# Late rows of segments 62 and 63 projected in the opening, feed-forward products in steps 58 to 60, and the tail's transfers in another order

## The chip, the cores and the metric

The kernel runs on one core of one Trainium2 chip. The metric is the device time of one execution in microseconds (us), as the median of several runs. One further execution was taken with the hardware profiler; its instruction trace and a page made from it are what "the profile" means here. The engines are TensorE (PE for its matmuls, PEld for its weight loads), VectorE (DVE), ScalarE (ACT), GpSimd (POOL) and SyncE (SP). SP issues most transfers (DMAs) from one queue in program order; they are moved by 16 transfer engines.

## The reference

Part A is a transformer layer over 64 segments of 32 tokens with a recurrent memory of 8 rows; part B is a gated feed-forward layer over all 2,048 tokens. Numbers are bf16, the width D is 640, there are 32 heads of 128, and F is 1,728.

```python
mem = mem0                                    # [8, 640]
for s in range(64):
    h = concat([mem, LN(x)[32 * s:32 * s + 32]])           # 40 rows
    q, k, v = h @ Wq, h @ Wk, h @ Wv                       # 32 heads of 128
    p = softmax(where(mask, q @ k.T * 128 ** -0.5, -1e9))  # memory rows see all, the others causally
    o = (p @ v) @ Wo                                       # back to 640
    mem, out[32 * s:32 * s + 32] = o[:8], o[8:]            # the memory of the next segment
h = x + out
z = LN(h)
result = h + (relu(z @ W_gate) * (z @ W_up)) @ W_down
```

The loop over s is sequential: a segment's memory rows come out of the segment before it.

## The kernel before

**Scheduling.** The kernel writes its operations in one list (`add`, `dma`) with the tiles that each reads and writes as keys. `solve` works out the semaphore waits from the keys. Each engine runs its own operations in the order of the list, and SP issues its transfers in that order too: a transfer that must wait holds all transfers behind it.

**A step.** Segment s is one pass of the loop `for s in range(1, NSEG)`; the opening does segment 0. Of a segment's 40 rows, 32 (8 memory rows and the first 24 tokens, the "act_r" rows) are projected in the step itself, as the stationary operand of 128x32, while 512 columns of the weights stream past; four such matmuls go into the four 32-column groups of the array. The last 8 tokens of a segment don't depend on the memory. They are collected for four segments at a time (`act_e`, 32 rows), and their K, Q and V are projected ahead, in three of every four steps. `extra_units(s)` gives such a step its 40 additional matmuls, which `filler(0..2)` spreads over the places in the step where the recurrence would leave TensorE idle, and an `evac` that brings the result from the PSUM banks BQ (0 and 1) to `Ke`, `Qe` or `Ve`. `place(s)` says which of two buffers, and which slot of four, a segment has. Segments 0 and 1 have slots 2 and 3 of buffer 1, whose other two slots are empty in the opening; 62 and 63 have slots 0 and 1 and get their late rows' K, Q and V in steps 58, 59 and 60. Step 61 projects segment 63's remaining queries.

`merge_v` copies V (`Vp`, `Ve`) into VM by transfers, since rows change partitions; `pv_x(s - 1)` reads VM in the step after. `store_attn` writes the rows of attention to `attn_d`. `fill_of(s)` splits some of a step's matmuls in two halves of 256 columns, or shares fewer weight loads, so that each step has a chosen number of TensorE instructions.

**Feed-forward.** Tokens go in four blocks of 512. The first block's normalised rows are made during the steps and kept in `xn2_d`; step 62 loads them into `xn2T[0]`. `gate_up(b, j)` is one pair for 128 of the F columns: five matmuls of the gate and five of up (128x128 stationary, 512 tokens streaming), then `relu` on ScalarE and the product on VectorE into `hT[b % 2][:, j]`; j = 13 is a tail of 64 columns in `Wt`. `down_pair` multiplies `hT` by `Wd`; its first part of a block reads j = 0 to 11 and so the first four `Wd` loads at once. Block 0's pairs j = 0 to 3 stand in and behind the last step, where they fill waits of the recurrence; j = 4 to 13 follow in the loop of block 0.

**The tail's transfers.** The feed-forward weights lie where Wq, Wk and Wv were, so they can be loaded only after the last projection by each (`Wdone`). `load_piece` takes the next of a list of column groups of gate and up (`GROUPS`: 0 to 255, 256 to 511, 512 to 1,023, 1,024 to 1,535, 1,536 to 1,663), and `load_down` a third of the rows of `Wd` at a time. Each is tied to a key such as `("hT", 0, j)`, the product of pair j, which sets when SP may issue it. `ln2_load`, `ln2_front` and `ln2_back` load, normalise and turn the rows of the next block.

## Time and profile before

| | us |
|---|---|
| median of 3 runs | 1000.11 (1000.02 to 1000.35) |
| the profiled execution | 999.84 |
| its span, first to last instruction or transfer | 998.1 |
| TensorE busy with matmuls | 974.4 (98% of the span) |
| VectorE, ScalarE, GpSimd busy | 713.6, 524.3, 167.4 |

Busy time of TensorE is modelled from pipelined matmuls, so a busy TensorE isn't one at its peak; the chain of waits says better what sets the end. In the rows of groups, "xN" is the count, then come the busy time and the mean of one instruction in ns, then idle time before it. In the timeline and the chain, the first two columns are start and length in us. In the tables of stretches the last columns are the granted clock of TensorE, the mean busy share of the transfer engines, and GB/s.

### The profile page before, as it was taken

What the parts mean: (1) busy time and instruction counts of PE and PEld (TensorE: products, weight loads), DVE (VectorE), ACT (ScalarE), POOL (GpSimd) and SP (SyncE); (2) the same over time, 40 slices, a digit from 0 to 9 for tenths busy, and PEclk for the clock granted to TensorE, in tenths of its full rate; (3) what the DMA queues carried; (4) which work ended last, traced back from release to release, by engine and by line L of the source; (5) the groups of instructions that cost most, each with busy time, mean ns of one, the idle gap of its engine ahead of it and who ended that gap; (6) DMA issues with size and microseconds to landing.
All of it is one profiled execution on the core that took longest, in us unless ns stands there. A gap on an engine that the chain in (4) does not pass through costs nothing.

```text
span 998.1 us, 56128 instructions
## 1 busy us (share of the span) xinstructions
PE 974.4 (98%) x26025; PEld 533.0 (53%) x24736; DVE 713.6 (71%) x1861; ACT 524.3 (53%) x1330; POOL 167.4 (17%) x414
## 2 busy tenths in 40 slices
PE   3899999999999999999999999999999999999998
PEld 1145555655555555555556565655555554344443
DVE  2568787878888887888788878787878766345332
ACT  0456666656666666666666566665656643122120
POOL 7021202021302130222022212121110010000000
PEclk9999999999999999999999999999999999999999
DMA  9931212121222122121212131112111169513100
GB/s 373 416 109 28 54 28 54 30 60 51 54 42 54 49 54 46 48 55 48 49 46 61 45 60 42 41 41 39 41 36 39 35 181 249 101 20 93 27 14 26
DMA packets 73534, 73.32 MB, mean 73 GB/s; under 512 B 42480, under 2 KB 60112, under 8 KB 71376
## 3 DMA queue, kind: packets, MB, share of 16 engines
q1 hardware_dynamic: 71568, 68.83, 25.0%
q8 instruction: 199, 3.26, 1.4%
q10 hardware_dynamic: 1728, 0.91, 0.3%
q14 instruction: 39, 0.32, 0.1%
HBM read 37.04 MB, written 6.55 MB: 44 GB/s over the span
## 4 chain that ended last, share of the span: by engine, by line
PE 94%; DMA 3%; DVE 1%; SPq 1%; issue 0%; ACT 0%; DVEq 0%; ACTq 0%
PE ps L394 47%; PE ps L858 11%; PE ps L367 8%; PE ps L582 7%; PE ps L599 7%; PE ps L642 4%; PE ps L1114 3%; DMA W<-in_A_Wv_dram 3%; PE ps L483 2%; PE ps L671 2%; PE ps L536 2%; SPq L332 1%; PE ps L871 0%; PE ps L1127 0%; PE ps L894 0%
## 5 line engine op out<-in xcount | busy, mean ns | idle before, releaser
L394 PE MATMUL ps<-W,act_r 128*32 128x512 bf16 (+1 forms) x8327 | 453.7, 357 | 1.7 <-ACT tok L418 0.9
L394 PEld LDWEIGHTS ps<-W,act_r 128*32 128x32 bf16 x8327 | 213.9, 96 | 165.7 <-DVE act_r L623 32.1
L418 ACT ACTIVATE tok<-ps 128x512 bf16<-128x512 f32 x190 | 109.3, 594 | 57.3 <-PE ps L394 48.7
L394 PE MATMUL ps<-W,act_e 128*32 128x512 bf16 x1224 | 119.5, 383 | 5.9 <-DVE TBf L464 3.4
L413 DVE STREAM_TRANSPOSE Ko<-tox 128x512 bf16<-128x512 bf16 x128 | 89.5, 700 | 40.1 <-ACT tox L418 39.7
L491 POOL COPY Qo<-Qe 128x256 bf16<-128x256 bf16 x64 | 27.8, 434 | 528.6 <-DVE oT L556 488.9
L418 ACT ACTIVATE tox<-ps 128x512 bf16<-128x512 f32 x134 | 79.6, 598 | 63.2 <-PE ps L394 42.5
L562 DVE STREAM_TRANSPOSE oT<-tox 128x512 bf16<-128x512 bf16 x128 | 95.6, 747 | 0.0
L413 DVE STREAM_TRANSPOSE Qo<-tok 128x512 bf16<-128x512 bf16 x124 | 85.5, 690 | 0.9
L367 PE MATMUL ps<-W,act_e 128*32 128x512 bf16 x856 | 84.1, 384 | 0.0
L582 PE MATMUL ps<-Wo,oT 128*32 128x160 bf16 x4032 | 81.4, 233 | 0.0
L599 PE MATMUL ps<-Wo,oT 128*32 128x320 bf16 x2016 | 79.8, 299 | 0.6 <-DVE rm L546 0.6
L582 PEld LDWEIGHTS ps<-Wo,oT 128*32 128x32 bf16 x4032 | 70.3, 97 | 11.0 <-DVE oT L556 3.1
L418 ACT ACTIVATE Vp<-ps 128x512 bf16<-128x512 f32 x127 | 75.2, 592 | 0.5 <-PE ps L858 0.5
L886 ACT ACTIVATE g<-ps 128x512 bf16<-128x512 f32 x52 | 30.1, 593 | 79.3 <-PE ps L858 79.3
L612 ACT ACTIVATE SA<-TA 64x40 f32<-64x40 f32 x126 | 29.5, 234 | 75.3 <-DVE TA L610 74.5
L499 ACT ACTIVATE Pm<-ps 128x64 bf16<-128x64 f32 x126 | 28.1, 223 | 73.0 <-PE ps L483 72.9
L858 PE MATMUL ps<-xn2T,Wg 128*128 128x512 bf16 x260 | 64.7, 380 | 0.0
L858 PE MATMUL ps<-xn2T,Wu 128*128 128x512 bf16 x260 | 64.6, 379 | 0.0
L887 DVE TENSOR_TENSOR hT<-g,ps 128x512 bf16<-128x512 bf16 x52 | 35.7, 686 | 40.3 <-PE ps L858 38.4
L599 PEld LDWEIGHTS ps<-Wo,oT 128*32 128x32 bf16 x2016 | 52.7, 97 | 16.8 <-DVE rm L546 1.3
L556 DVE STREAM_TRANSPOSE oT<-om 128x128 bf16<-128x128 bf16 x126 | 39.0, 310 | 31.1 <-ACT om L548 31.1
(114 smaller groups left out, 1447.0 us busy)
## 6 DMA issues: line engine op xcount, KB each, us to landing
VM<-Vp SPq DMA_DIRECT2D x126, 65.0 KB
VM<-Vp SPq DMA_DIRECT2D x63, 130.0 KB
W<-in_A_Wk_dram SPq DMA_DIRECT2D x5, 1024.0 KB
W<-in_A_Wq_dram SPq DMA_DIRECT2D x5, 1024.0 KB
W<-in_A_Wv_dram SPq DMA_DIRECT2D x5, 1024.0 KB
Wo<-in_A_Wo_dram SPq DMA_DIRECT2D x8, 640.0 KB
attn_d<-wtok SPq DMA_DIRECT2D x248, 7.5 KB
xt<-in_A_x_dram SPq DMA_DIRECT2D x16, 160.0 KB
```

The source lines that it names most:

```text
L367: return pe.add_instruction(mybir.InstMatmult(name=nc.get_next_instruction_name(), engine=mybir.EngineType.PE, ins=[pe.lower_ap(rhs), pe.l ...
L394: ins = pe.matmul(*b, start=(c == ends[0]), stop=(c == ends[1]), skip_group_check=True)
L413: add("dve", lambda v: v.transpose(dst[:, 16 * i:16 * i + 16, 0:32], tok[t][:, :].rearrange("p (h f) -> p h f", f=32)), r=tok_keys(t), w=keys)
L418: add("act", lambda a: a.activation(dst, src, ACTF.Copy), r=r, w=w)
L556: add("dve", lambda v: v.transpose(ap(oT[par], 160 * hf, [[40, 4], [320, 4], [1, 8]]), ap(om, 128 * hf, [[1, 4], [4, 32]])), r=[("om", hf) ...
L562: add("dve", lambda v, kh=kh: v.transpose(ap(oT[p], 160 * kh + M, [[320, 4], [40, 4], [1, 32]]), ap(tox, 128 * kh, [[256, 4], [1, 4], [4, ...
L582: i = pe.matmul(bank(bk)[32 * gg:32 * gg + 32, 0:160], src[:, hb, 0:32], w[:, gg], start=(hb == CH[16 * halves[0]]), stop=(hb == CH[-1]), ...
L599: i = pe.matmul(bank(bk)[32 * q:32 * q + 32, 0:320], src[:, hb, 0:32], w, start=(n == 0), stop=(n == 7), skip_group_check=True)
L642: ins = pe.matmul(bank(bk)[32 * q:32 * q + 32, 0:320], src[:, hb, 0:32], w[:, 2 * (q % 2):2 * (q % 2) + 2], start=(i == 0), stop=(i == 15) ...
L858: ins = pe.matmul(bank(bk), w[:, c, lo:lo + 128], xn2T[par][:, c, :], start=(c == 0), stop=(c == DC - 1))
L886: add("act", lambda a: a.activation(g1[gi][:, :], bank(bg), ACTF.Relu), r=[B(bg)], w=[("g1", gi)])
L887: add("dve", lambda v: v.tensor_tensor(hT[par][:, j, :], g1[gi][:, :], bank(bu), ALU.mult), r=[B(bu), ("g1", gi)], w=[("hT", par, j)])
```

## The change

1. **Late rows.** `place` gives segments 0 and 1 slots 0 and 1 of buffer 1, and segments 62 and 63 slots 2 and 3. The opening loads the last 64 rows of x behind the first 64 in `xt`, normalises 128 rows, and puts the late rows of all four segments into `act_e[1]`. So the opening's projections give K, Q and V of the late rows of 62 and 63 too. Step 1 stores the buffer (`ends`, which now holds `Ke[1]`, `Qe[1]` and `Ve[1]` side by side) to `ends_d`; step 61 loads it back. One of the four loads of the memory moves from ACT's queue to SP's.
2. **Early products.** In steps 58 to 60 `extra_units` returns `early_product`: the gate and up products of block 0 for one j of 0, 1, 2 each. The normalised rows are loaded into `ends` in step 57, the weights into `xt` and `xl` (one j at a time), and the result goes to `hx_d`, which the tail loads into `hT`. These matmuls, and those of block 0's j = 3 to 6, go in four groups of 32 columns (`by_groups`). `fill_of` has new numbers for steps 58 to 60.
3. **Tail.** Block 0's pairs in and behind the last step are j = 3 to 6 in place of 0 to 3, and its loop has seven pairs (j = 7 to 13, counted as p = 4 to 10) in place of ten. The column groups are 384 to 639, 640 to 895, 896 to 1,407, 1,408 to 1,663, and last 0 to 383. `Wt`, `Wd`, the rows of h, the weights of columns 0 to 383 and the rows of block 1 are asked for at other pairs than before.

The core of the diff:

```diff
+    ends_d = nc.dram_tensor("ends_d", [128, 64 * H + 8 * VW], BF16)
+    NE = 3
+    hx_d = nc.dram_tensor("hx_d", [128, NE, TB], BF16)
...
-    Ke = [ar.alloc(f"Ke{i}", [128, H, 32], BF16) for i in range(2)]
+    ends = ar.alloc("ends", [128, 64 * H + 8 * VW], BF16)
+    Ke = [ar.alloc("Ke0", [128, H, 32], BF16), _Part(ends, 0, (H, 32))]
     Qo = ar.alloc("Qo", [128, H, M + SEG], BF16)
-    Qe = [ar.alloc(f"Qe{i}", [128, H, 32], BF16) for i in range(2)]
-    Ve = [ar.alloc(f"Ve{i}", [128, 8, VW], BF16) for i in range(2)]
+    Qe = [ar.alloc("Qe0", [128, H, 32], BF16), _Part(ends, 32 * H, (H, 32))]
+    Ve = [ar.alloc("Ve0", [128, 8, VW], BF16), _Part(ends, 64 * H, (8, VW))]
...
         if b < 0:
             for e in range(2):
-                copy(act_r[1][:, 2 + e, :, M:32], src[:, :, SEG * e:SEG * e + RID], [("act", 1, "x", 2 + e)])
-                copy(act_e[1][:, :, M * (2 + e):M * (3 + e)], src[:, :, SEG * e + RID:SEG * e + SEG], [("acte", 1)])
+                copy(act_r[1][:, e, :, M:32], src[:, :, SEG * e:SEG * e + RID], [("act", 1, "x", e)])
+            copy(act_e[1][:, :, :].rearrange("p c (e t) -> p c e t", t=M),
+                 src[:, :, :].rearrange("p c (e t) -> p c e t", t=SEG)[:, :, :, RID:SEG], [("acte", 1)])
...
     def place(s):
+        if s < 2 or s >= NSEG - 2:
+            return 1, s % 4
         return (s - 2) // 4 % 2, (s - 2) % 4
...
-    ln1_load(-1, xt, ("xt",), "act")
+    for n, t0 in enumerate((0, S - 64)):
+        dma(xt[64 * n:64 * n + 64, :], x_ap[t0:t0 + 64, :], w=[("xt", "late") if n else ("xt",)], eng="act")
     ln1_load(0, x0, ("oTe", 0), "act")
-    for g in range(4):
+
+    def mem_load(g, eng):
         dma(wtok[32 * g:32 * g + M, :, :],
-            mem0_ap.rearrange("t (c g j) -> g t c j", g=4, j=32)[g], r=[("wtok",)], w=[("wtok0", g)], eng="act")
+            mem0_ap.rearrange("t (c g j) -> g t c j", g=4, j=32)[g], r=[("wtok",)], w=[("wtok0", g)], eng=eng)
+
+    for g in range(3):
+        mem_load(g, "act")
     srcs = (A_Wq, A_Wk, A_Wv)
     for j in (1, 0, 2):
         for c in range(DC):
             dma(W[:, j, c, :], srcs[j][128 * c:128 * c + 128].rearrange("p h e -> p (h e)"), w=[("W", j, c)])
+            if j == 1 and c == 0:
+                mem_load(3, "sp")
...
+    EC = 128 * NE
+    GROUPS = ((EC, EC + 256), (EC + 256, EC + 512), (EC + 512, EC + 1024), (EC + 1024, FM), (0, EC))
     pieces = [(t, n, src, g, lo, hi) for g, (c0, c1) in enumerate(GROUPS)
               for n, (t, src) in enumerate(((Wg, B_W_gate), (Wu, B_W_up)))
-              for lo, hi in (((0, 3), (3, DC)) if c1 - c0 == 512 else ((0, DC),))]
+              for lo, hi in (((0, 3), (3, DC)) if g in (2, 4) else ((0, DC),))]
...
+    END_KEYS = [("Ke", 1, 0), ("Ke", 1, 1), ("Qe", 1, 0), ("Qe", 1, 1), ("Ve", 1, 0), ("Ve", 1, 1), ("Ve1", 1)]
+    XHOME = [(ends[:, 512 * c:512 * c + 512], END_KEYS[c]) for c in range(DC)]
+    HOME, HKEY = ends[:, 64 * H + 4 * VW + 8:64 * H + 4 * VW + 520], END_KEYS[DC]
+
+    def by_groups(pe, dst, w, x, c):
+        for g in range(4):
+            ins = pe.matmul(dst[32 * g:32 * g + 32, :], w[:, 32 * g:32 * g + 32], x, start=(c == 0), stop=(c == DC - 1),
+                            skip_group_check=True)
+        return ins
+
+    def early_rows(lo, hi):
+        dma(ends[:, 512 * lo:512 * hi].rearrange("p (c t) -> p c t", t=512), xn2_d[:, lo:hi, :],
+            r=[("xn2_d", u) for u in range(4)], w=END_KEYS[lo:hi] + ([("Ve1", 1)] if hi == DC else []))
+
+    def early_weights(j, q):
+        t, k, src = ((xt, ("xt",), B_W_gate), (xl, ("xl",), B_W_up))[q]
+        dma(chunks_of(t[:, :]), src[:, 128 * j:128 * j + 128].rearrange("(c p) f -> p c f", p=128), w=[k])
+
+    def early_product(s, n):
+
+        def mul(q, chunks):
+            t, k = ((xt, ("xt",)), (xl, ("xl",)))[q]
+
+            def f(pe):
+                for c in chunks:
+                    ins = by_groups(pe, bank(BQ[q]), chunks_of(t[:, :])[:, c, :], XHOME[c][0], c)
+                return ins
+            add("pe", f, r=[k] + [XHOME[c][1] for c in chunks], w=[B(BQ[q])])
+
+        def part(m):
+            mul(*((0, range(DC)), (1, range(1)), (1, range(1, DC)))[m])
+
+        def evac():
+            add("act", lambda a: a.activation(HOME, bank(BQ[0]), ACTF.Relu), r=[B(BQ[0])], w=[HKEY])
+            add("dve", lambda v: v.tensor_tensor(HOME, HOME, bank(BQ[1]), ALU.mult), r=[B(BQ[1]), HKEY], w=[HKEY])
+            dma(hx_d[:, n, :], HOME, r=[HKEY], w=[("hx", n)])
+        return part, evac
...
+        elif 2 <= s < NSEG - 3 and r < 3:
             j = (1, 0, 2)[r]
             a, ks = act_e[p], [("acte", p)]
-            if s < 0 or (s - 2) // 4 + 1 > (NSEG - 2) // 4:
-                return None, None
+            if (s - 2) // 4 + 1 == (NSEG - 2) // 4:
+                return early_product(s, r)
...
+                    if b == 0 and j < NE + 4:
+                        ins = by_groups(pe, bank(bk), w[:, c, lo:lo + 128], xn2T[par][:, c, :], c)
+                        continue
...
-        n = {1: 31, 2: 8, 57: 39, 61: 39, 62: 50, 63: 0}.get(s, FILL[s % 4])
+        n = {1: 31, 2: 8, 57: 39, 58: 0, 59: 27, 60: 40, 61: 39, 62: 50, 63: 0}.get(s, FILL[s % 4])
...
+            if NSEG - 6 < s < NSEG - 3:
+                early_weights(s - NSEG + 6, 1)
+            elif s == NSEG - 3:
+                for n in range(2):
+                    dma(ends[:, 1024 * n:1024 * n + 1024], ends_d[:, 1024 * n:1024 * n + 1024], r=[("ends",)],
+                        w=END_KEYS[2 * n:2 * n + 2])
+            elif s == 1:
+                dma(ends_d[:, :], ends[:, :], r=END_KEYS, w=[("ends",)])
...
+            if s == NSEG - 7:
+                early_weights(0, 0)
+                G.ops[-1].after = first_exp
+                early_rows(2, 4)
+            elif s == NSEG - 3:
+                dma(ends[:, 2048:], ends_d[:, 2048:], r=[("ends",)], w=END_KEYS[4:])
...
+        if s == NSEG - 7:
+            early_rows(0, 2)
+            early_rows(4, DC)
+            early_weights(0, 1)
+        elif NSEG - 6 <= s < NSEG - 4:
+            early_weights(s - NSEG + 7, 0)
...
     rows(P3, s % 2, s - 1)
-    gate_up(0, 1)
+    gate_up(0, NE + 1)
     load_piece(("VM", 0, 3))
-    load_piece(("hT", 0, 0))
+    load_piece(("hT", 0, NE))
     pv_x(s, P0)
     norm_x(P0)
     norm_x_late(P0)
     flip_ox(s)
     late_o(s)
-    load_piece(("hT", 0, 1))
-    gate_up(0, 2)
+    load_piece(("hT", 0, NE + 1))
+    gate_up(0, NE + 2)
     ln2_load(4)
-    load_piece(("hT", 0, 2))
-    load_piece(("hT", 0, 2))
-    gate_up(0, 3)
-    load_piece(("hT", 0, 3))
-    load_piece(("hT", 0, 3))
+    load_piece(("hT", 0, NE + 2))
+    load_piece(("hT", 0, NE + 2))
+    gate_up(0, NE + 3)
+    load_piece(("hT", 0, NE + 3))
+    dma(hT[0][:, 0:NE, :], hx_d[:, :, :], r=[("Wdone", 2), ("hT", 0, NE + 3)] + [("hx", n) for n in range(NE)],
+        w=[("hT", 0, n) for n in range(NE)])
     rows(P2, (s + 1) % 2, s)
     ln2_load(5)
     woe_pass(P3, range(16))
...
         if 0 < b < NBLK - 1:
             for u in range(4):
                 ln2_load(4 * (b + 1) + u)
-        at0 = 5 if b == 0 else 1
         for j in range(FC):
-            if b or j > 3:
+            p = j - NE if b == 0 else j
+            if b or p > 3:
                 gate_up(b, j)
-            if b == 0 and 4 <= j < 7:
-                load_piece(("hT", 0, j))
-            if b == 0 and j in (5, 7):
-                ln2_load(6 + (j - 5) // 2)
-            if b == 0 and 4 <= j < 9:
-                load_down(j - 4)
-            if b == 0 and j == 5:
+            if b == 0 and p == 4:
                 for q, src in enumerate((B_W_gate, B_W_up)):
                     for e in range(2):
                         r0 = FR * (q ^ e)
                         dma(Wt[:, e, :, r0:r0 + FR], src[:, FM:F].rearrange("(c p) f -> p c f", p=128),
-                            r=[("Wdone", 0), ("hT", 0, 5)], w=[("Wt", q, e)])
-            if b == 0 and j == 9:
+                            r=[("Wdone", 0), ("hT", 0, j)], w=[("Wt", q, e)])
+            if b == 0 and p in (5, 7):
+                ln2_load(6 + (p - 5) // 2)
+            if b == 0 and 4 <= p < 8:
+                for n in ((0,), (1, 2), (3,), (4,))[p - 4]:
+                    load_down(n, p)
+            if b == 0 and p == 6:
                 dma(h_rows[0][:, :, :], h_d[:, :].rearrange("(u p) d -> p u d", p=128), r=[("h_d", u) for u in range(4)] +
-                    [("Wdone", 1), ("hT", 0, 9)], w=[("h", 0, u) for u in range(4)])
+                    [("Wdone", 1), ("hT", 0, j)], w=[("h", 0, u) for u in range(4)])
+            if b == 0 and p in (8, 9):
+                load_piece(("hT", 0, j))
+                load_piece(("hT", 0, j))
             if b + 1 < NBLK:
-                if j - at0 in (0, 2, 4, 6):
-                    ln2_front(4 * (b + 1) + (j - at0) // 2)
-                if j - at0 - 2 in (0, 2, 4, 6):
-                    ln2_back(4 * (b + 1) + (j - at0 - 2) // 2, None)
+                fronts, backs = ((4, 6, 8, 10), (6, 8, 10, 10)) if b == 0 else ((1, 3, 5, 7), (3, 5, 7, 9))
+                if p in fronts:
+                    ln2_front(4 * (b + 1) + fronts.index(p))
+                for n in range(4):
+                    if p == backs[n]:
+                        ln2_back(4 * (b + 1) + n, None)
         assert not pieces
         for n in range(2):
             down_pair(b, n)
```

40 lines of the change are left out of this document (24 added, 16 removed).

## The prediction

> **What bounds the kernel now.** I read the page first, then the chain of waits of the whole run, then the timeline and tables of stretches of the three places that the change touches: the opening, steps 57 to 61, and the tail.
>
> ```profile
> span 998.1 us, 56128 instructions
> PE 974.4 (98%) x26025; PEld 533.0 (53%) x24736; DVE 713.6 (71%) x1861; ACT 524.3 (53%) x1330; POOL 167.4 (17%) x414
> PE 94%; DMA 3%; DVE 1%; SPq 1%; issue 0%; ACT 0%; DVEq 0%; ACTq 0%
> ```
>
> TensorE is 94% of the chain that ended last. So matmuls taken out of its stream come off the end, unless something is late at the place where they were. The chain's pieces (start, length, what) price them:
>
> ```profile
> 12.12 28.10 DMA W<-in_A_Wv_dram
> ...
> 809.89 2.27 PE ps L858 x10
> ...
> 814.68 2.26 PE ps L858 x10
> ...
> 826.18 19.53 PE ps L858 x90
> ...
> 845.71 1.09 PE ps L871 x10
> ```
>
> L858 is `gate_up`: ten matmuls of 512 columns make one pair. Nine pairs of block 0 in a row took 19.53 us, 2.17 us each. The single pairs in the last step took 2.26 and 2.27. The one DMA piece is the opening: the chain stands on a load of Wv until 40.22 us.
>
> **The pairs.** `GROUPS` and the loop over `p` leave block 0's gate and up products for j = 0 to 2 out of the tail; their results come back from `hx_d`. Off the chain: 3 x 2.17 = 6.51 us. In their place `early_product` puts 20 gate and 20 up matmuls of 32 columns into each of steps 58 to 60, where the late rows of segments 62 and 63 were projected:
>
> ```profile
> L394 PE MATMUL ps<-W,act_e 128*32 128x512 bf16 x72 | 7.0, 379 | 0.0
> ...
> L367 PE MATMUL ps<-W,act_e 128*32 128x512 bf16 x48 | 4.7, 379 | 0.0
> ...
> 746.73 0.35 PE ps L671 x32
> ...
> 758.77 0.35 PE ps L671 x32
> ...
> 770.81 0.35 PE ps L671 x32
> ...
> 808.81 1.08 PE ps L394 x20
> ```
>
> The first two rows, groups of 746.6 to 782.8 us, are the old work: 120 matmuls of 128x512 in 32 columns, 40 a step, as many as the new. A run of 20 such matmuls, each with its own weights, took 1.08 us in the chain (last row), so 40 take 2.16: one full pair. The new forty need 40 weight loads where the old shared 24; the split halves (`fill_of`: 7, 52, 56 become 0, 27, 40) shrink by 48, as much as the loads grow. The steps with 7 and 52 splits both last 12.04 us (the three L671 rows). I take 0 for both edits. ScalarE and VectorE get less: one activation and one product in place of two copies and up to two flips.
>
> Here a rule speaks against the change. The Trainium skill, "TensorE: Matmul & The Clock Gate", Part 3, gives 2.38x for three column tiles of N=512, short of 3x. By it the four pairs that also go into groups in the last step (j = 3 to 6) would take 3/2.38 of 2.17 us, an estimate of 2.3 us more in all; the 1.08 us row speaks against that, and I go by the row. The groups rather save something: the lone pairs' 2.27 and 2.26 stand 0.1 above 2.17 where 32-column work turns to 128-column work. Bounds 0 and 0.4 us, I take 0.2 off.
>
> **The opening.** The 64 late rows are added to `xt` (80 KB); their columns in the late-row batches were empty, so no matmul is added.
>
> ```profile
> 13.50:27.00 13.50, 9.74 (x136) 2.05 (x68) 2.98 (x10) 2.20 (x5) 9.54 (x50) 1.00 1.01 418
> ...
> 6.57 0.88 DVE L336 BATCH_NORM_STATS2 st<-xt 64x6 f32<-64x320 bf16 x2 [4.97 <-DMA xt<-in_A_x_dram]
> ...
> 16.40 0.33 DVE L420 CAST ps<-wtok 128x160 f32<-128x160 bf16 x1 [2.24 <-DMA wtok<-in_A_mem_dram]
> ...
> 40.26 0.40 PE L394 MATMUL ps<-W,act_e 128*32 128x512 bf16 x4 [1.67 <-DMA W<-in_A_Wv_dram]
> ```
>
> The transfer engines are full (share 1.01, 418 GB/s, the last two columns of the first row), and TensorE waits 1.67 us for Wv at 40.26. So 80 KB more push everything by 82 KB/418 GB/s = 0.2 us. The second half of `xt` may be later than 6.57 by a microsecond or so; behind it VectorE still waits 2.24 us for `wtok` at 16.40, and TensorE has the 1.67 in hand, so that is hidden. If that cover failed it would cost up to 1 us. The memory row moved from ACT's queue to SP's passes the queue's first W load alone. The store of `ends` (128 x 6,176 bytes, 790 KB) stands behind the last Wo and `xl` loads on SP's queue and before the flip of step 1; it costs 1.9 us of a queue that nothing in step 1 waits on yet. I take 0.2 for the opening, bounds 0 and 1.
>
> **Steps 57 to 61, the SP queue.** Here new transfers stand before the copies of V (VM), which `pv_x` of the next step reads.
>
> ```profile
> 738.69 0.22 ACT L499 ACTIVATE Pm<-ps 128x64 bf16<-128x64 f32 x1 [0.49 <-PE ps L483]
> ...
> 740.75 1.80 SPq L332 DMA_DIRECT2D VM<-Vp  x3
> ...
> 746.66 0.42 PE L671 MATMUL ps<-VM,Px 64*32 64x129 bf16 x32
> ...
> 752.89 0.22 PE ps L394 x4
> ...
> 756.55 2.22 PE ps L394 x43
> ...
> 764.07 0.22 PE ps L394 x4
> ...
> 765.32 0.22 PE ps L394 x4
> ...
> 994.76 1.18 SPq L332 DMA_DIRECT2D out_dram<-osb  x2
> ```
>
> In step 57 `early_weights(0, 0)` (160 KB) and `early_rows(2, 4)` (256 KB) go ahead of VM. VM's three are issued by 742.55 and read at 746.66, 4.1 us. On a quiet queue a transfer takes about 2.2 us (the last store is issued by 995.94, the span ends at 998.1). 426 KB at the 207 GB/s of the slowest row quoted below are 2.1 us, and they start after the exponential of 738.69, two microseconds before VM: covered, by some 2 us. The weights for steps 59 and 60 are asked for when the matmuls that read their buffer are done: the gate's after those that end at 753.1 now, for use at 764.07, the up's after those that end at 756.55, for use at 765.32. That is 11 and 8.8 us; the up weights stand behind a `hx_d` store that waits for the product, which leaves them some 7. The restore of `ends` in step 61 waits for the last `hx_d` store and stands before that step's VM, which is due some 7 us later. Nothing in this cover is thin; for disturbance of the kind that a busy queue makes I put 0.2 us, bounds 0 and 2.
>
> **The tail.** With three pairs fewer, block 0's down products begin 6.5 us earlier, and their weights must keep up.
>
> ```profile
> Wd<-in_B_W_down_dram SPq DMA_DIRECT2D x4, 480.0 KB
> xt<-in_A_x_dram SPq DMA_DIRECT2D x16, 160.0 KB
> at<-attn_d SPq DMA_DIRECT2D x16, 160.0 KB
> h<-h_d SPq DMA_DIRECT2D x1, 640.0 KB
> Wt<-in_B_W_gate_dram SPq DMA_DIRECT2D x2, 80.0 KB
> Wt<-in_B_W_up_dram SPq DMA_DIRECT2D x2, 80.0 KB
> Wd<-in_B_W_down_dram SPq DMA_DIRECT2D x1, 160.0 KB
> ...
> 828.48 0.69 DVE L887 TENSOR_TENSOR hT<-g,ps 128x512 bf16<-128x512 bf16 x1 [1.25 <-PE ps L858]
> ...
> 846.64 0.30 PE L1114 MATMUL ps<-Wd,hT 128*128 128x320 bf16 x1
> ...
> 849.90 0.30 PE L1114 MATMUL ps<-Wd,hT 128*128 128x320 bf16 x1
> ...
> 830.00:834.00 4.00, 4.00 (x20) 1.86 (x19) 2.62 (x6) 1.20 (x5) 0.00 (x0) 1.00 0.96 280
> ...
> 837.00:841.00 4.00, 4.00 (x20) 1.77 (x19) 3.04 (x7) 1.51 (x4) 0.00 (x0) 1.00 0.91 207
> 841.00:845.00 4.00, 4.00 (x20) 1.85 (x19) 2.91 (x7) 1.51 (x4) 0.00 (x0) 1.00 1.15 290
> 829.20:846.64 17.44, 17.44 (x88) 8.34 (x86) 12.18 (x27) 5.87 (x16) 0.00 (x0) 1.00 0.96 250
> ```
>
> In the new order the four `Wt`, all of `Wd` 0 to 3 and one `ln2_load` are asked for from the product of j = 7 on, which ends where j = 4's does now (829.17): 320 + 1,920 + 320 KB = 2.62 MB. The first down part reads hT 0 to 11 and thus `Wd` 0 to 3 at once; now it starts at 846.64, then at 840.1. At 280 GB/s (830 to 834) the last byte is there at 829.2 + 2.2 + 9.4 = 840.8; at 290 (841 to 845, mostly `Wd`) at 840.4; at the mean of 250 at 841.9; at 207 at 844.0. So a first wait of 0.3 to 3.9 us. Then the 13th chunk needs the fifth `Wd`, 24 matmuls later, 849.90 - 846.64 = 3.26 us; before it lie `h`, an `ln2_load` and its own 160 KB, 1.15 MB: 4.0 us at 290, 4.1 at 280, 4.6 at 250, 5.6 at 207, so 0.7 to 2.3 us more. Sum: 1.0 at 290, 1.5 at 280, 3.1 at 250, 6.2 at 207; if transfers overlap better than in any of these rows, 0. I take 1.2, between the two rows in which long rows of `Wd` prevail, since the new order asks for the four big ones nearly in a run; the low row holds the `Wt` loads of short rows and a stall of SP's queue. What goes out of this stretch helps: the four halves of columns 0 to 383 come after `Wd`, for block 1 only. The load of `hx_d` (384 KB) comes before 829, where the columns from 1,408 on now take 640 KB (two arrays of 640 rows by 256) in place of 1,280 (by 512).
>
> Sum on the profiled execution (999.84 us, span 998.1): -6.5 - 0.2 + 0.2 + 0.2 + 1.2 = -5.1, so 994.7. The median shown is 1000.11, 0.27 above that execution; from it, 995.0.
>
> **The rivals.** *Nothing waits in the tail*: `Wd` is there in time and the sum is -6.3, 993.8. For it: the big transfers come in a run. Against: the transfer engines are at a share of 0.91 to 1.15 all through.
>
> *The tail is bound by its transfers*: the rate stays at its mean of 250 GB/s or falls to 207, the wait is 3.1 to 6.2 us, and the kernel ends at 996.9 to 1000.0. For it: the same mix moves now at 250. Against: part of that mean is the queue's own stall.
>
> *The groups are slow* (the skill's rule above, as a mechanism): 20 matmuls of 32 columns would have to take 1.36 us in place of 1.08, and the end would be 997.3. No run of such matmuls in this trace does that.
>
> *Slower*: the early products wait for their operands inside the recurrence. They stand ahead of `pv_mem` and of the next step, so each microsecond of lateness in a step is one on the chain. The shortest cover is that of the up weights, 7 us. To turn -5.1 into more than +2.0, steps 59 and 60 must each be 3.6 us late, so a load of 160 KB must take 10.6 us instead of about 3: 164 KB in 8.4 us after the 2.2 of latency, 20 GB/s, against 207 in the slowest busy row. At 4.2 us late a step the end is at 1003.4. Rows of 256 bytes speak for it a little; the Trainium skill, "DMA: Bandwidth & Descriptors", Specifications, asks for 512 bytes or more for full rate.
>
> *It doesn't do what it says*: the late rows need no new matmul, and the pairs do leave the loop; I see no way to this.
>
> **How the numbers follow.** Forecast, 994.2 to 996: 0.55. Nothing waits, down to 993.2: 0.14. Bound by transfers: 0.19, of it 0.06 above 998.1. Slow groups: 0.04. Slower, by that mechanism or another stall of its size: 0.08. A measurement of this kernel tells 0.2%, 2.0 us, from no change: faster is below 998.1, slower above 1002.1. Faster 0.55 + 0.14 + 0.13 + 0.04 = 0.86, same 0.06, slower 0.08. The range 993.2 to 997.7 holds the first two cases, most of the third's lower part and the groups: 0.83.
>
> **What would show it.** Right: in the chain, six pairs in a row before the tails piece in place of nine; steps 58 to 60 still 12.04 us from one L671 row to the next; TensorE's first matmul on Wv's fourth chunk at about 40.4; a wait of TensorE on `Wd` of about 1 us, in one or two pieces, before or among the L1114 matmuls of block 0. Wrong: L671 or the early matmuls waiting for a DMA in steps 58 to 60; runs of 20 grouped matmuls above 1.2 us; a wait on `Wd` over 3 us; a new wait in block 1, on `xn2T` or on the columns 0 to 383.

## The result and the profile after

The changed kernel takes 998.14 us (median of 19 executions, 996.3 to 999.8), the kernel before 1000.23 beside it: a ratio of 0.9978, interval 0.9971 to 0.9985. It is 2.1 us faster. A second measurement gave 997.43 against 1000.07 (0.9973, 0.9963 to 0.9984), 2.6 us. The forecast was 5.1 us. The profiled execution of the changed kernel took 996.77 us, among the fastest of its runs.

First the page of the kernel after, then pieces of its chain of waits (start, length, what):

```profile
span 995.0 us, 56301 instructions
PE 967.6 (97%) x26077; PEld 530.5 (53%) x24848; DVE 711.5 (72%) x1856; ACT 521.2 (52%) x1324; POOL 166.9 (17%) x412
PE 93%; DMA 3%; SPq 2%; DVE 1%; issue 0%; ACT 0%; POOL 0%; DVEq 0%; ACTq 0%; POOLq 0%
```

```profile
747.66 0.35 PE ps L692 x32
...
759.70 0.35 PE ps L692 x32
...
771.73 0.35 PE ps L692 x32
...
783.76 0.35 PE ps L692 x32
...
810.92 2.17 PE ps L832 x40
...
815.58 2.16 PE ps L832 x40
...
827.02 6.44 PE ps L928 x29
...
835.84 3.12 SPq L372
839.01 0.59 SPq L349
839.64 5.94 DMA at<-attn_d
845.61 0.50 DVE h L724
846.21 0.30 PE ps L1204
```

L692 is `pv_x` (L671 before), L832 is `by_groups`, L928 is `gate_up` at 128 columns, L1204 is `down_part`. TensorE's busy time fell by 6.8 us, but the end only by 3.1. The chain no longer runs on TensorE alone through the tail: it steps onto SP's queue and a transfer. The waits themselves stand in TensorE's timeline (start, length, what; in brackets the wait before it and what ended it):

```profile
40.90 0.40 PE L411 MATMUL ps<-W,act_e 128*32 128x512 bf16 x4 [1.65 <-DMA W<-in_A_Wv_dram]
...
59.75 0.42 PE L692 MATMUL ps<-VM,Px 64*32 64x129 bf16 x32
...
842.24 0.30 PE L1204 MATMUL ps<-Wd,hT 128*128 128x320 bf16 x1 [1.24 <-DVE hT L957]
...
846.21 0.30 PE L1204 MATMUL ps<-Wd,hT 128*128 128x320 bf16 x1 [0.55 <-DVE h L724]
```

The engines named as releasers had long been done or were done just then; the fourth `Wd` load landed at 842.15 and the fifth at 846.08. And the end, VectorE's last addition in the kernel before and after, and SP's closing waits (minimum, median and maximum length in ns; first and last start), before and after:

```profile
995.25 0.33 DVE L1136 TENSOR_TENSOR osb<-ps,h 128x160 bf16<-128x160 f32 x1 [0.52 <-PE ps L1114]
```

```profile
991.56 0.33 DVE L1226 TENSOR_TENSOR osb<-ps,h 128x160 bf16<-128x160 f32 x1 [0.52 <-PE ps L1204]
```

```profile
L1263 SPq EVENT_SEMAPHORE  x24: 17/28/279, 996.0 to 997.6; - x24
```

```profile
L1358 SPq EVENT_SEMAPHORE  x24: 17/28/28, 992.3 to 994.6; - x24
```

The last addition comes 3.69 us earlier, the last closing wait only 3.0.

The difference of the two spans, place by place, with the forecast's term (`pv_x` of step 1 starts at 59.11 before and 59.75 after, of step 63 at 807.00 and 807.91):

| place | forecast | these two traces |
|---|---|---|
| opening, to `pv_x` of step 1 | +0.2 | +0.64 |
| steps 1 to 62 | +0.2 | +0.27 |
| step 63 and what fills it, to 826.18 and 827.02 | -0.2 | -0.07 |
| from there to the first down product, without its wait (20.46 and 13.98 us) | -6.5 | -6.48 |
| wait ahead of the first down product | | +1.24 |
| the second wait and the rest, to VectorE's last addition | +1.2 (both waits) | +0.71 |
| from there to the end | 0 | +0.6 |
| sum | -5.1 | -3.1 |

The pairs and the early products went as forecast: steps 58 to 60 take 12.04, 12.03 and 12.03 us, and TensorE waits for nothing in them. What is missing in this execution is in the opening (0.4 us), the tail's waits (0.8) and the end (0.6). The median is a further microsecond short of the forecast, and this trace can't show where: other executions are slower than this one by a microsecond or more.

### The profile page after: what moved, and what is told of

It is laid out like the page before. It is cut to its first block, busy times and chain, and to the rows that moved or that the text cites. A ratio compares the mean times of both kernels' runs of the same rounds, so it can differ in the third digit from the quotient of the medians.

```text
span 995.0 us, 56301 instructions
## 1 busy us (share of the span) xinstructions
PE 967.6 (97%) x26077; PEld 530.5 (53%) x24848; DVE 711.5 (72%) x1856; ACT 521.2 (52%) x1324; POOL 166.9 (17%) x412
## 4 chain that ended last, share of the span: by engine, by line
PE 93%; DMA 3%; SPq 2%; DVE 1%; issue 0%; ACT 0%; POOL 0%; DVEq 0%; ACTq 0%; POOLq 0%
PE ps L411 47%; PE ps L928 9%; PE ps L384 8%; PE ps L603 7%; PE ps L620 7%; PE ps L663 4%; PE ps L1204 3%; DMA W<-in_A_Wv_dram 3%; PE ps L504 2%; PE ps L692 2%; PE ps L557 2%; PE ps L832 2%; SPq L349 1%; DMA at<-attn_d 1%; PE ps L941 0%
## 5 line engine op out<-in xcount | busy, mean ns | idle before, releaser
L435 ACT ACTIVATE tok<-ps 128x512 bf16<-128x512 f32 x186 | 107.2, 594 | 56.8 <-PE ps L411 48.7
L411 PE MATMUL ps<-W,act_e 128*32 128x512 bf16 x1152 | 113.1, 384 | 5.5 <-DMA W<-in_A_Wv_dram 4.1
L384 PE MATMUL ps<-W,act_e 128*32 128x512 bf16 x808 | 80.1, 386 | 0.0
L504 PE MATMUL ps<-Qo,Ko 128*32 128x40 bf16 x2048 | 61.2, 181 | 0.0
L957 DVE TENSOR_TENSOR hT<-g,ps 128x512 bf16<-128x512 bf16 x49 | 33.6, 687 | 38.6 <-PE ps L928 34.1
L504 PEld LDWEIGHTS ps<-Qo,Ko 128*32 128x32 bf16 x2048 | 46.0, 94 | 26.2 <-DVE Qo L430 18.8
L1204 PE MATMUL ps<-Wd,hT 128*128 128x320 bf16 (+4 forms) x225 | 57.9, 299 | 1.8 <-DVE hT L957 1.2
```

The source lines that it names most:

```text
L384: return pe.add_instruction(mybir.InstMatmult(name=nc.get_next_instruction_name(), engine=mybir.EngineType.PE, ins=[pe.lower_ap(rhs), pe.l ...
L411: ins = pe.matmul(*b, start=(c == ends[0]), stop=(c == ends[1]), skip_group_check=True)
L435: add("act", lambda a: a.activation(dst, src, ACTF.Copy), r=r, w=w)
L504: i = pe.matmul(bank((P0, P1)[hf])[q:q + 32, o:o + 40], (Ko if a == 0 else Ke[p])[:, h, :], Qo[:, h, :], start=True, stop=True, skip_group ...
L1204: i = pe.matmul(*a, start=(j == 0), stop=(j == FC - 1), skip_group_check=True)
```

## The experiments

All edits are to the changed kernel, and "faster" and "slower" are against its second measurement, 997.43 us; the kernel before took 1000.07 to 1000.41 beside the four sets of runs. A chunk of `Wd` is one of its first five loads, and "the load ahead" is the one that SP issued just before the second chunk. "Apart" below is the time from the first to the last of the 16 transfer engines to complete one load, from the trace's completion records.

**The changed kernel again.**

> The changed kernel, unchanged, once more. Its 19 runs lay in three groups, spans of 994.5 to 995.7, 995.7 to 996.8 and 997.8 to 998.1 us, while the kernel before kept within 0.9 us; the profiled execution (996.77) is from the low end, the median is 998.14. Theory A: the spread is made in the tail, by waits on loads whose landing changes from run to run; another execution then shows waits on Wd other than 1.24 and 0.55 us, and all else up to step 63 as in the first trace to 0.3 us. Theory B: the spread is made elsewhere, in the granted clock or in the steps; then the marks of the steps differ between the two traces by a like amount, and the waits on Wd stay at about 1.8 us together. Both expect a median of 997 to 998.5 us and the spread again.

997.43 us (996.54 to 998.27). In its trace the waits on `Wd` are 0.84 and 0.56 us instead of 1.24 and 0.55 us; `pv_x` of step 1 is at 60.09 instead of 59.75, of step 63 at 808.03 instead of 807.91. So two places vary, the opening by 0.3 us and the tail's waits by 0.4. Both theories have a part: in this trace the granted clock was also 0.5 from 35.7 to 39.2 us, in the opening.

**The memory's row back on ACT's queue.**

```diff
-    for g in range(3):
+    for g in range(4):
         mem_load(g, "act")
...
-            if j == 1 and c == 0:
-                mem_load(3, "sp")
```

> The fourth load of the memory's rows goes back from the SP queue, where it stands behind the first weight load, to ACT's. Theory A: the opening's +0.64 us (forecast: +0.2) comes from that load's issue of 0.88 us on SP, which moved every later weight load by 0.6 to 0.9 us; PE then meets Wv's fourth chunk at 40.4 to 40.5 us instead of 40.90, and the whole is 0.4 us faster than the changed kernel. Rival: the 80 KB of late rows on the queue take the time whichever engine issues; the chunk is met at 40.8 to 41.0 and the time is the same within 0.1 us. It might also return a wait on the memory's rows, which landed last on ACT's queue: then +0.1 to +0.5 us.

998.92 us (0.9986 of before, 0.9977 to 0.9995), 1.5 slower than the changed kernel instead of 0.4 faster. Wv's fourth chunk landed at 40.91: the rival's number. Steps 1 and 62 took 12.43 and 12.46 us instead of 12.10 and 12.16. That isn't the wait on the memory's rows that the expectation's last sentence feared, as those rows landed long before step 1; why the two steps are longer is not known. The rest lies in the tail: this execution waited 2.36 us on `Wd`, and then the granted clock fell. That the edit makes the tail worse is not shown, since the tail's waits vary from one execution to the next. The table of stretches (busy times by engine, then the granted clock, the transfer engines' share and GB/s):

```profile
842.00:844.00 2.00, 0.06 (x1) 0.09 (x1) 1.45 (x4) 0.46 (x2) 0.00 (x0) 1.00 2.11 267
844.00:846.00 2.00, 2.00 (x9) 0.57 (x5) 0.07 (x1) 0.00 (x0) 0.00 (x0) 0.52 0.48 126
846.00:848.00 2.00, 2.00 (x11) 0.61 (x5) 0.00 (x0) 0.00 (x0) 0.00 (x0) 0.62 1.09 310
848.00:850.00 2.00, 2.00 (x17) 0.71 (x8) 1.59 (x4) 0.14 (x1) 0.00 (x0) 1.00 1.35 247
```

TensorE did 9 and 11 matmuls in 2 us where it does 17 at full clock. The clock was at half for 3.4 us, so 1.7 us were lost behind a wait of 2.4.

**Wt's loads at the start of step 63.** The four loads move from p = 4 of the tail to `if last:` ahead of the first projection, without the wait on a product.

> The four loads of Wt, 2.3 us of SP's issue time and about 2 us of the queue just ahead of Wd's first chunk, are issued at the start of step 63 instead, where the SP queue has nothing to issue for 4 us. Everything that follows in the tail's queue comes up to 2 us earlier. Theory A: the two waits of PE on Wd (1.24 to 1.39 and 0.55 to 0.87 us) are a matter of the queue's length; they shrink to under 0.3 us together, the time falls by 1.8 to 2.3 us against the changed kernel, and if they also make the spread, its runs lie within 1 us of each other. Rival: the waits are set by SP's stall in the transposes (3.12 us) and not by the bytes ahead; the first goes, the second stays or grows, and the gain is 0.7 to 1.4 us, the spread as it was. Either way the early loads could delay step 63's own transfers: then +0.2 to +1 us at its start.

995.56 us (994.87 to 996.10), 1.9 faster than the changed kernel. One wait is left:

```profile
844.46 0.30 PE L1210 MATMUL ps<-Wd,hT 128*128 128x320 bf16 x1 [0.47 <-DVE h L724]
```

The gain is theory A's, the spread of 1.2 us a little over it; of the waits the first went and the second stayed, as the rival had it. Why the move is worth so much stands in SP's issues and in the stretches of the changed kernel, and in the same stretch of the last run below, which has loads of long rows in `Wt`'s place (second fence):

```profile
829.88 1.14 SPq L349 DMA_DIRECT2D Wt<-in_B_W_gate_dram  x2
831.06 1.10 SPq L349 DMA_DIRECT2D Wt<-in_B_W_up_dram  x2
832.20 0.53 SPq L349 DMA_DIRECT2D Wd<-in_B_W_down_dram  x1
...
830.00:834.00 4.00, 4.00 (x20) 1.84 (x19) 3.00 (x7) 1.51 (x4) 0.00 (x0) 1.00 0.65 98
834.00:838.00 4.00, 3.95 (x19) 1.79 (x19) 3.00 (x8) 1.52 (x4) 0.00 (x0) 1.00 0.98 341
838.00:842.00 4.00, 3.01 (x19) 1.67 (x17) 3.20 (x8) 1.36 (x4) 0.00 (x0) 1.00 1.04 354
```

```profile
830.00:834.00 4.00, 4.00 (x21) 1.77 (x19) 3.01 (x8) 1.51 (x4) 0.00 (x0) 1.00 0.32 93
```

Issuing the four loads takes SP 2.3 us, so `Wd`'s first chunk is issued at 832.20; with `Wt` early it is issued at 829.60, and the fourth chunk lands at 839.45 instead of 842.15. From 830 to 834 only 98 GB/s moved. With the same bytes in long rows it was 93 GB/s at a share of 0.32: the transfer engines were two thirds idle, so the time goes into SP's issues, neither into the bytes nor into short rows. The move also left a pause: the second chunk's issue is tied to the next product, and from 833.7 to 834.7, ahead of its bytes, the queue moved only 41 GB/s.

**The closing waits in order of last use.**

```diff
-        self.dma_end = {s: o.count for s, o in sem_last.items()}
+        at = {op.sem: n for n, op in enumerate(self.ops) if op.dma}
+        self.dma_end = {s: sem_last[s].count for s in sorted(at, key=at.get)}
```

> SP's waits for the 48 DMA semaphores at the end of the program are put in the order of each semaphore's last use, so that the semaphore of the last store is waited for last. Theory A: in the changed kernel 20 waiting instructions of about 61 ns stand behind the one for the last store (9 before), which is the 0.59 us by which the end of the span grew; with the order by last use none is left behind it, and the time falls by 20 x 61 ns = 1.2 us against the changed kernel (0.6 is the least). Rival: the time from the last store to the end is set by the store's own landing and by fixed work after it; the time is the same within 0.2 us.

996.49 us (996.03 to 997.93), 0.9 faster. In its trace VectorE's last addition ends at 993.66, and the closing waits are

```profile
L1359 SPq EVENT_SEMAPHORE  x24: 17/28/28, 994.1 to 995.5; - x24
```

The last of them comes at 995.5: 1.8 us from addition to last wait, against 2.7 in the changed kernel and 2.0 before. So the end's +0.6 was the order of these waits: the semaphores go round by 48, and the number of transfers decides how many waiting instructions stand behind that of the last store. The tail waited 1.57 and 1.39 us here.

**Block 1's first transposing transfer later.**

```diff
-                fronts, backs = ((4, 6, 8, 10), (6, 8, 10, 10)) if b == 0 else ((1, 3, 5, 7), (3, 5, 7, 9))
+                fronts, backs = ((4, 6, 8, 10), (7, 8, 10, 10)) if b == 0 else ((1, 3, 5, 7), (3, 5, 7, 9))
```

> One number of the changed kernel's order: block 1's first transposing transfer is issued after the fifth Wd chunk's load instead of right behind h's. In the traces so far its issue holds SP for 3.12, 3.49, 4.11 and 4.81 us, and in the same time Wd's second to fourth chunk land late: the waits of PE on Wd are 1.79, 1.40, 2.96 and 2.36 us in those four; in the one where the queue was 2 us shorter the issue took 1.60 us and the waits 0.47 us. Theory A: the transposing transfer, queued behind about 2 MB of loads, slows the loads while it is being issued, and keeps SP from the fifth chunk; issued later, it lets the chunks land at 1.2 us each from 837 us, the fourth by 841; both waits are under 0.3 us, the time falls by 1.5 to 2.5 us against the changed kernel, and the runs lie within 1 us. Rival: the loads are slow by themselves (memory), and the long issue is their consequence: the first wait stays at 0.8 to 2.4 us, only the second goes, and the gain is under 0.8 us.

996.66 us (995.65 to 1000.6), 0.8 faster, as the rival had it. The second wait is gone, the first is

```profile
843.06 0.30 PE L1204 MATMUL ps<-Wd,hT 128*128 128x320 bf16 x1 [2.20 <-DMA Wd<-in_B_W_down_dram]
```

2.20 us, although SP issued the transposing transfer only at

```profile
837.45 2.33 SPq L349 DMA_DIRECT2D Wd<-in_B_W_down_dram  x3
839.83 1.86 SPq L372 DMA_TRANSPOSE xn2T<-xt  x1
```

839.83, by when the second chunk should long have been there. It landed at 840.31, its engines 2.85 us apart. The transposing transfer is not what makes the chunks late.

**Three edits together** (Wt early, the transposing transfer later, the closing waits in order).

> Three edits together on the changed kernel: Wt's loads at the start of step 63, the transposing transfer after the fifth Wd chunk, and the end's waits in the order of last use. If they act apart: no wait on Wd is left (the run with Wt early kept 0.47 us), and the end is 0.86 us shorter; from the 995.6 us of Wt early that gives 994.2 to 994.9. Rival: with Wt early the transposing transfer no longer costs anything, and the fifth chunk's wait is on the last rows of attn; then 994.7 to 995.2.

993.54 us (993.27 to 993.72; 0.9933 of before, 0.9921 to 0.9945), better than both kernels and than expected. No wait on `Wd` of 0.3 us or more is left, and the five executions lie within 0.45 us.

**Products at 128 columns again in block 0.** `by_groups` is left out of `gate_up`; steps 58 to 60 keep it.

> The seven product pairs of block 0 behind step 62 that run in 32-column groups go back to 128 columns; the pairs of steps 58 to 60 keep their groups, and all else stays. Theory A (the forecast's term): in groups a chunk costs what it costs at 128 columns, and the only gain is the time lost where PE changes the width between products and projections: 0.2 us, at most 0.4, so 0.0 to 0.4 us slower than the changed kernel, no more than its spread. Rival (groups dear): this kernel is faster by over 0.5 us. The pairs' duration in the trace decides: 2.16 us for 40 grouped matmuls so far.

997.75 us (996.76 to 998.96), 0.3 slower than the changed kernel's 997.43, inside both spreads. In the chain the pairs are as before the change, with an "issue" of 0.16 us ahead of each:

```profile
810.99 0.16 issue
811.15 2.10 PE ps L928 x9
...
815.77 0.16 issue
815.93 2.10 PE ps L928 x9
```

2.26 us with the change of width, against 2.17 and 2.16 in groups. The groups are not dear; they save 0.1 us where they stand alone. By the 2.38x of the Trainium skill, "TensorE: Matmul & The Clock Gate", Part 3, they would cost about 0.6 us more each, an estimate; the 2.17 and 2.16 us here speak against it.

**The kernel before again.**

> The kernel before, once more, for a second trace of its opening, tail and end. In the changed kernel and its variants Wv's fourth chunk landed at 40.70 to 41.56 us in five traces, against 40.22 in the one trace of before. Theory A: the change costs the opening 0.5 to 1.0 us; here the chunk lands within 0.3 us of 40.22. Rival: the landing varies by as much in both kernels and the opening costs the forecast 0.2 us; here it lands at 40.5 to 41.3. Block 1 of before starts without a wait on Wd in both.

1000.06 us. The chunk landed at 40.32: theory A. The landing varies little in this kernel; the change costs the opening 0.4 to 1.3 us (40.64 to 41.56 in eight traces).

**Long rows in Wt's place, first try.**

> As the run with Wt early, and in the place where Wt's four loads were, four loads of the same 80 KB each of Wd's first rows into the output buffers, which nothing uses then: bytes as before, but rows of 1280 B instead of 128 B, so 256 rows instead of 2560. In six traces with Wt in its place, Wd's second chunk landed 2.0 to 3.9 us behind the load ahead of it (1.2 us at full rate), with the 16 DMA engines up to 2.9 us apart; in the two with Wt early, where the queue had run empty before that chunk, they stayed within 0.5 us. Theory A: it is the queue that is never empty, with about 2 MB behind one another, whatever the rows; the engines come apart here too, the first wait on Wd is over 0.8 us and the time within 0.6 us of the changed kernel's 997.4 to 998.1. Rival: it is Wt's many short rows; here the engines stay together, the chunks land about 0.5 us later than with Wt early, waits are under 0.8 us and the time is 995.3 to 996.3.

1002.33 us (999.88 to 1004.07), which neither expected. Two loads each went to one buffer under the same keys, so they waited for one another, and `Wd`'s first chunk was issued at 836.2 instead of 832.2. It says nothing of the bytes. The second chunk's engines were 1.97 us apart without any short rows.

**The fourth chunk asked for with the fifth.** `((0,), (1, 2), (3,), (4,))` becomes `((0,), (1, 2), (), (3, 4))`.

> One move in the changed kernel: Wd's fourth chunk is loaded with the fifth, behind h's, the transposing transfer and two loads of rows, so that PE waits for it longer: about 4 us where it waited 0.8 to 2.4. Asked is what a longer wait costs beside itself. In one trace a wait of 2.36 us was followed by a granted clock of 0.50 to 0.75 for 3.4 us, about 1.7 us of work lost; behind waits of up to 2.2 us in five others the clock stayed at 1.00. Theory A: a wait of that length always lowers the clock behind it; the trace shows 0.5 for 3 to 4 us behind the wait, the granted clock is 0.997 or 0.998 in every run, and the time is 4 + 1.7 - 2 = 3.7 us above the changed kernel's, 1001 to 1002.5. Rival: the clock fell by chance there; it stays at 1.00 and the time is 999.5 to 1000.5.

1004.83 us (1003.70 to 1005.12). The wait was 7.08 us, not 4, and behind it:

```profile
844.00:846.00 2.00, 0.00 (x0) 0.00 (x0) 0.00 (x0) 0.00 (x0) 0.00 (x0) 0.76 1.08 334
846.00:848.00 2.00, 0.05 (x1) 0.08 (x1) 1.59 (x4) 0.10 (x1) 0.00 (x0) 0.50 1.09 303
848.00:850.00 2.00, 2.00 (x8) 0.63 (x5) 0.45 (x1) 0.40 (x2) 0.00 (x0) 0.50 1.28 207
850.00:852.00 2.00, 2.00 (x9) 0.55 (x4) 0.00 (x0) 0.00 (x0) 0.00 (x0) 0.54 1.14 310
852.00:854.00 2.00, 2.00 (x17) 0.69 (x7) 0.00 (x0) 0.00 (x0) 0.00 (x0) 1.00 0.51 112
```

half the clock until 851.8 (a mean of 0.54 from 850 to 852 is half for 1.84 of the 2 us), from TensorE's return at 847.95 on 3.9 us: 1.9 us of work lost beside the wait. The fall itself came at 845.0, while TensorE still waited. The mean granted clock was 0.995 to 0.997 in all four executions, and 0.995 to 0.998 in all ten of the run before this one, whose wait was 4.77 us. Theory A's mechanism holds; it missed the wait's length by 3 us, and so the time (1001 to 1002.5) by over 2.

**The opening without the late rows**, with zeros in their place, the memory on ACT's queue (first) or on SP's (second):

```diff
-    for n, t0 in enumerate((0, S - 64)):
-        dma(xt[64 * n:64 * n + 64, :], x_ap[t0:t0 + 64, :], w=[("xt", "late") if n else ("xt",)], eng="act")
+    dma(xt[0:64, :], x_ap[0:64, :], w=[("xt",)], eng="act")
+    add("dve", lambda v: v.memset(xt[64:128, :], 0.0), w=[("xt", "late")])
```

> The changed kernel with the opening's transfers as before the change: the late rows' load is left out (DVE fills the rows with zeros, so the last two segments are computed from zeros), and the fourth load of the memory's rows is on ACT's queue. Wv's fourth chunk landed at 40.22 and 40.32 us in two traces of the kernel before, at 40.64 to 41.56 in eight of the changed one and its variants, 40.91 with the late rows and the memory on ACT. Theory A: the transfers alone set it; it lands at 40.1 to 40.5 here. Rival: something else in the new opening (the first 128-row moments, the copies) does; then 40.6 or later, although no weight load waits for those.

> The same with the fourth load of the memory's rows left on the SP queue, where the change put it: the late rows' 80 KB are gone, the move is kept. Theory A (the forecast's terms, and the memory's place without cost, as its return to ACT bought nothing): Wv's fourth chunk lands 0.2 us earlier than in the changed kernel's traces, at 40.5 to 40.8. Rival 1: the late rows cost more than their bytes; it lands at 40.1 to 40.4, as before the change. Rival 2: the move costs all of it; 40.8 to 41.0.

The chunk landed at 40.34 and 40.28: the transfers set it. The late rows cost all of the 0.4 to 1.3 us, and the move of the memory's row to SP's queue costs nothing (rival 1 of the second). The runs, 998.65 and 998.30 us, are no faster than the changed kernel all the same: `pv_x` of step 1 is at 59.67 and 59.61, behind a stall of VectorE that no other trace has, and the waits on `Wd` were 2.53 and 1.83 us, two waits each, none over 1.31. The stall in the second of the two:

```profile
57.08 0.20 DVE L644 TENSOR_TENSOR act_r<-TBf,SA 128x40 bf16<-128x40 f32 x1 [0.54 <-DVE TBf L643]
```

The zeros are one VectorE instruction more ahead of it. That the shift of the instructions by one put the stall there is likely and not shown.

**What pulls the transfer engines apart.** Two more runs:

> The version with all three edits, but Wd's second and third chunk no longer wait for the ninth chunk's product: they are issued right behind the rows of attn, at about 831 us instead of 832.9, while the queue still holds the loads ahead. In two traces where the queue ran empty for 0.7 us ahead of the second chunk, the 16 engines landed it within 0.5 us of each other; in eight where it did not, they were 1.2 to 2.9 us apart. Theory A: a queue that goes on without a pause is what pulls the engines apart; here they are over 1 us apart in the second or third chunk, but with 2 us more lead the time is within 0.5 us of 993.5. Rival: the pause has nothing to do with it; the engines stay within 0.6 us, the fourth chunk lands at 838 to 838.5 instead of 839.8, and the time is 993.2 to 993.6.

994.51 us (993.95 to 994.54). Theory A's mechanism: the second chunk's engines are 2.85 us apart, and it lands at 838.70, 2.1 later than in the version of the three edits, though it was issued 1.2 earlier. The time missed both: it is 1.0 above 993.54. In the trace, 0.74 us of lateness is there before `pv_x` of step 63 (808.25 against 807.51), so only about 1.4 of the 2.1 belong to the load.

> The run with long rows as it was meant: Wt early, and in its old place four loads of 80 KB in rows of 1280 B, which do not wait for one another. Issue of Wd's first chunk at about 832, as in the changed kernel. Theory A (no pause in the queue, whatever the rows): Wd's second chunk lands 2 us or more behind the load ahead of it, its engines over 1 us apart, the first wait is 0.6 to 2.4 us, the time 996.5 to 998.5. Rival (Wt's short rows): engines within 0.6 us, the chunk 1.2 to 1.4 us behind the load ahead, the fourth at 840.5 to 841, waits under 0.8 us together and 995.3 to 996.3.

997.73 us (996.46 to 999.86). Theory A: 2.24 us apart, 3.05 behind the load ahead, waits of 2.02 and 0.43.

| trace | load ahead landed | second chunk, first to last engine | fourth chunk | from load ahead to fourth chunk |
|---|---|---|---|---|
| changed kernel | 836.96 | 837.76 to 838.96 | 842.15 | 5.19 |
| again | 836.86 | 837.77 to 839.27 | 841.88 | 5.02 |
| transposing transfer later | 836.61 | 837.46 to 840.31 | 842.97 | 6.36 |
| long rows, second try | 837.58 | 838.39 to 840.63 | 843.22 | 5.64 |
| three edits, no pause | 834.95 | 835.85 to 838.70 | 841.41 | 6.46 |
| Wt early (a pause) | 834.14 | 836.36 to 836.74 | 839.45 | 5.31 |
| three edits (a pause) | 834.08 | 836.14 to 836.60 | 839.82 | 5.74 |

In all twelve traces in which the queue went on without a pause into the second chunk, its engines were 1.2 to 3.2 us apart; in the two with a pause, 0.4 and 0.5. Neither short rows nor the transposing transfer is needed. A queue without a pause isn't always enough either: in the two traces of the kernel before, where the second and third chunk are issued while other loads still move, their engines are 1.1 and 0.5, and 1.6 and 0.9 us apart. What slows some engines is not settled. The last column shows what it costs: where the engines are 2.9 us apart, the fourth chunk lands 6.4 and 6.5 us behind the load ahead, where they are 1.2 to 1.5 apart, 5.0 to 5.2. With the pause it is 5.3 and 5.7, as the pause itself takes about a microsecond. So the two traces with a pause are early because their load ahead landed 2.8 us sooner, without `Wt` in front of it.

## Why the prediction was wrong

**Pairs, early products, groups: right.** -6.48 for -6.5; 12.03 us a step; 40 grouped matmuls in 2.16. The rival of slow groups and the slower rival (products that wait in steps 59 and 60) did not occur. That the 0.2 us for steps 57 to 61 met +0.27 is luck: from `pv_x` of step 57 to that of step 62 it is 60.23 us against 60.20, and the rest lies in earlier steps.

**The tail: the step that failed most.** It was "I take 1.2, between the two rows in which long rows of `Wd` prevail". The waits were 1.79 and 1.40 us in the two traces of the changed kernel, 1.83 to 2.96 in five variants with the same order of loads, 2.1 in the mean of the seven (both waits together). Two things were wrong in it. The lowest row was set aside because it holds the `Wt` loads and a stall of SP's queue, but the new order has the same four `Wt` loads at its head. The working counts them by their bytes, 1.2 us at 280 GB/s; in SP's queue they took 2.1 to 2.3 us to issue, and without them the fourth chunk landed 2.7 us sooner (0.3 of it because that trace was ahead before `pv_x` of step 63). The rival "bound by its transfers" had this right: from 829.9 to 842.2 us the seven traces moved 240 to 264 GB/s, its row said 250, and its band of 996.9 to 1000.0 holds the median. But its wait of 3.1 was not reached, and the rate was not low throughout: behind 834 it was 277 to 379 GB/s.

The other thing is that the working treated the queue as one stream with a rate. A load has landed when its slowest engine is done, and the 16 engines don't stay together. By the formula, counted from SP's first `Wt` issue in each trace, the fourth chunk was due 11.6 us later at 280 GB/s; in these seven traces it landed 0.3 to 1.8 us behind that. The Trainium skill, "DMA: Bandwidth & Descriptors", on why a DMA increments its semaphore by 16, says that the engines finish independently and only the full count means landed; the first and last completions above agree. A mean of GB/s can't show it.

**The clock was not in the sum.** In the tail, behind single waits of up to 2.20 us the clock stayed at 1.00; with waits of 2.36, 4.77 and 7.08 it fell to half, for 3.4 us with the first and 6.8 with the other two, of which 5.6 and 3.9 us lay behind TensorE's return. So these waits cost 1.7, 2.8 and 1.9 us more than their length. The Trainium skill, "TensorE: Matmul & The Clock Gate", Part 1, has half and full rate alone, and half after an idle window of about 3.4 us; the two rates agree, but one wait of 2.36 was enough here. Four of the 19 executions of the first measurement, those with the longest spans (997.8 to 998.1), have a mean clock of 0.997 or 0.998. That the same happened in them is likely and not shown, as they have no trace; a low mean alone isn't proof, since one of the fast executions (996.89) has 0.998 too, and in the second trace the clock fell in the opening, behind several waits for loads of 1.0 to 1.3 us.

**The opening: mis-sized.** "82 KB/418 GB/s = 0.2 us" was 0.4 to 1.3, most often 0.6. With the memory's row on SP, which makes the second weight load's issue follow the late rows', that load landed at 9.5 to 10.2 us in eleven traces, against 9.2 to 9.3 in the two of before and the two without the rows; with it on ACT it landed at 9.31, and the time was lost among the later loads. Even the first engine to complete Wv's fourth chunk did so 0.3 to 0.7 us later than without the rows. That the rows cost about three times their bytes is shown; why is not.

**The end: not priced.** The sum had no term behind the last addition. The prediction took the 2.2 us from the last store's issue (995.94) to the end of the span for a transfer's latency. By its completion records that store landed at 997.10; the last 1.0 us is SP's closing waits and the program's end. 18 transfers more (701 for 683) moved the last store's semaphore in the round of 48, and 0.6 us with it.

Put right, the tail and the end bring the time back: with `Wt`'s loads early, the transposing transfer out of the way and the closing waits in order the kernel is 6.6 us faster than before, with the late rows still in its opening.

## What to carry to other kernels

When work is taken out ahead of loads, count the issue time of every load that stands ahead of them in the queue, not its bytes alone: four loads of 80 KB kept SP busy for over 2 us ahead of the big ones here, and were better asked for earlier. Look when the last of the transfer engines completes a load, not at a mean rate. Where a forecast wait of TensorE comes near 2.4 us, look at the granted clock behind it; here that was another 1.7 to 2.8 us. A change of the number of transfers can move the end of the kernel through the order of its closing waits.

## What the runs showed that was not expected

- In the version of the three edits, a load issued 1.2 us earlier, with no pause ahead of it, landed 2.1 us later (1.4 without what the trace had lost before).
- Each closing wait instruction of SP takes about 61 ns from start to start (24 in 1.4 us, 994.1 to 995.5), which made 0.6 us of the result.
- With one more VectorE instruction ahead of it, a stall of 0.54 us stood in the path to step 1, about as large as what the late rows had cost.
